# Long GpSimd operations moved to VectorE and ScalarE, modulation weights as overlapping 128-row tiles, and a new order, in an adaLN block with dilated sliding attention

## The chip, the cores and the metric

The kernel runs on one core of one Trainium2 chip. Its five engines are TensorE (PE, matmuls), VectorE (DVE), ScalarE (ACT), GpSimd (POOL) and SyncE (SP); transfers run on DMA queues that SP and ACT issue. The metric is device time in microseconds (us) of one execution; lower is better. Three runs of the kernel before took 187.68 to 190.51 us, median 189.6.

## What is computed

`x` has 2048 rows of D = 448 bf16 values. A condition vector `c` (1 x 448) gives six modulation vectors.

```python
mod = (silu(c) @ w_mod).reshape(1, 6, 1, 448)     # sa, ca, ga, sb, cb, gb
h = layernorm(x) * (1 + ca) + sa
q, k, v = heads(h @ wqkv)                         # 16 heads of 28
# each position attends to 8 positions: itself and 2, 4, ... 14 before it
x = x + ga * (softmax(q k^T / sqrt(28)) v @ wo)
h = layernorm(x) * (1 + cb) + sb
x = x + gb * (silu(h @ w1) @ w2)                  # 448 -> 1792 -> 448
```

## The kernel before

The rows are split by parity (even and odd positions never attend to each other) into two sequences of NP = 1024, and these into NC = 4 chunks of 256. A first stage loads everything, takes the layer norm of each pair of 128-row tiles (`n10` to `n17`; `n1m` is pair m), transposes and modulates it into `hT` (`h0` to `h3` by chunk), and projects q and k (`qk<chunk><group>`) and v (`v0` to `v8`). Attention runs over nine units u of two blocks of 57 queries and 64 keys: logits `lg`, two exponentials `ex`, a mask `mk` on VectorE that multiplies the 1824 values of each row, weighted sums `av`, a reciprocal `rc` and a product `on`, a DMA transpose `otr` on SP, and a copy `al` that places the result in `oT`. Then follow the output projection `wo0` to `wo7` with its residual `res`, the second norms `n20` to `n27`, and the feed-forward part in four steps `s0` to `s3`: `f1` (448 to 1792, SiLU on ACT) and `f2` (1792 to 448), with the sum `ya` and the store `sto`.

TensorE works with pairs of 64-row halves: each projection has a part `S`, a GpSimd no-op that signals its end, and a part `C`. Four PSUM tiles of two banks (`ps`) are shared by all stages; whoever wants one waits for the reader of its last content.

The order of all 640 operations is written out by hand in the table `ORDER`: a number is the operation, the letter its engine (p TensorE, v VectorE, a ScalarE, g GpSimd, s SyncE). Each engine executes its own in that order, so an operation that waits holds up all that stand behind it on that engine. `hT` and `oT` are two ranges of one tile `ho`, so an `al` copy and a projection that follows it in the table also wait for each other.

At the start the modulation weights `w_mod` lie as four blocks of KM = 112 rows. The weights of q and k arrive in two halves, `ldwqk0` (row blocks 0, 1) and `ldwqk1` (2, 3); `pad0` to `pad3` copy them into `wp` with 32 columns per head; `mod1` is the matrix product that gives sa and ca. The first projection needs all four pads, the four modulations `h00.mod0`, `h00.mod1`, `h01.mod0`, `h01.mod1`, and so all of that. GpSimd does the small norm steps (`rstd`: one or two operations on 128 x 2 values, `nm`, `mean`), the signals, and before the change also two pads, two of nine `al` copies, one of two gatings of `wo` (`wog0`) and four of seven gatings of `w2` (`w2g`), which multiply the weights by ga and gb. Second norms take their sums from the residual (`accum_out`), and the squares on ACT (`HOW2`, "s"); first norms use VectorE's batch-norm statistics ("b").

Of the kernel before, what the change touches and what calls it, by code (L numbers as in the profile page):

```python
# [882 lines left out]
```

## Time and profile before

| | |
|---|---|
| three runs | 187.68, 189.6, 190.51 us |
| the profiled execution, its own time | 186.92 us |
| its span (first to last instruction) | 185.1 us |
| TensorE busy in the span | 162.3 us (88%) |
| VectorE, ScalarE, GpSimd busy | 93.7, 96.2, 44.7 us |
| mean granted TensorE clock | 0.979 |

Busy times say how long an engine executed, and not what the kernel waited for. For that the stretches in which TensorE sat idle are looked at, what ended each, and what that operation had waited for itself. A time such as 39.42 is a start counted from the span's begin.

### The profile page before, as it was taken

The page shows a single profiled execution, that of the slowest core. Times are in us where ns is not written, and L with a number is a line of the kernel's source. Part 1 is how long each engine was busy: PE and PEld are TensorE (multiplying, and loading weights), DVE is VectorE, ACT ScalarE, POOL GpSimd, SP SyncE. Part 2 cuts the span into 40 slices and gives each one's busy share as a digit, 9 for nine tenths or more (in the row PEclk, how much of TensorE's full clock was granted, in tenths as well). Part 3 has the DMA queues.
Part 4 walks back from the last instruction along what each step waited for, and adds up shares of the span by engine and source line. Part 5 has one row for each costly group of instructions (what it writes and reads, how often), then busy time and mean ns, then how long its engine had stood idle before and what let it go on. Part 6 is the DMA issues. An engine that isn't in the chain of part 4 may idle for free.

```text
span 185.1 us, 6152 instructions
## 1 busy us (share of the span) xinstructions
PE 162.3 (88%) x2713; PEld 84.8 (46%) x2713; DVE 93.7 (51%) x194; ACT 96.2 (52%) x128; POOL 44.7 (24%) x91
## 2 busy tenths in 40 slices
PE   7979799677868989879999999999999999999910
PEld 2344354354334545545556644455444445554700
DVE  2879999679557858993327484032062000002620
ACT  2140598725259657586698785585338854200000
POOL 6346434551100059432304202000400000000000
PEclk9999999997899999999999999999999999999995
DMA  5993599999687956434003343900009000000132
GB/s 176 339 360 84 96 200 239 110 132 119 210 62 197 212 199 31 89 75 102 0 0 60 64 104 68 109 0 4 0 3 259 4 0 4 0 0 4 50 102 66
DMA packets 33114, 18.20 MB, mean 98 GB/s; under 512 B 25016, under 2 KB 32568, under 8 KB 33080
## 3 DMA queue, kind: packets, MB, share of 16 engines
q1 hardware_dynamic: 30752, 14.92, 40.7%
q10 hardware_dynamic: 2328, 2.81, 4.9%
q8 instruction: 23, 0.38, 0.9%
q14 instruction: 11, 0.09, 0.2%
HBM read 9.86 MB, written 1.84 MB: 63 GB/s over the span
## 4 chain that ended last, share of the span: by engine, by line
PE 70%; DVE 8%; DMA 6%; POOL 5%; ACT 3%; issue 2%; DVEq 0%; POOLq 0%; ACTq 0%
PE ps L682 23%; PE ps L707 20%; PE ps L473 10%; PE ps L653 5%; DMA wqk<-in_A_wqkv_dram 4%; PE ps L490 4%; PE ps L719 3%; PE ps L602 2%; PE ps L528 2%; POOL rs L372 2%; DMA x_all<-in_A_x_dram 2%; DVE xn L387 1%; ACT ho L236 1%; DVE st L356 1%; DVE p L586 1%
## 5 line engine op out<-in xcount | busy, mean ns | idle before, releaser
L707 PE MATMUL ps<-w,both 64*128 64x448 bf16 x392 | 38.9, 349 | 0.0
L687 ACT ACTIVATE both<-ps 128x1024 bf16<-128x1024 f32 x28 | 27.8, 1022 | 17.6 <-PE ps L682 17.2
L473 PE MATMUL ps<-ho,wp 64*128 64x512 bf16 x224 | 26.9, 385 | 3.9 <-POOL ho L623 1.4
L682 PEld LDWEIGHTS <-w 64*128 64x128 bf16 x392 | 20.0, 94 | 22.5 <-issue 1.0
L707 PEld LDWEIGHTS <-both 64*128 64x128 bf16 x392 | 19.0, 94 | 17.6
L682 PE MATMUL ps<-h,w 64*128 64x512 bf16 x196 | 22.5, 376 | 0.6 <-ACT v L495 0.6
L682 PE MATMUL ps<-wqk,w 64*128 64x512 bf16 x196 | 22.3, 376 | 0.0
L661 DVE SCALAR_TENSOR_TENSOR x_all<-ps,x_all 128x448 bf16<-128x448 f32 x16 | 9.3, 621 | 22.6 <-PE ps L653 22.6
L473 PEld LDWEIGHTS <-wp 64*128 64x128 bf16 x224 | 11.3, 95 | 17.3 <-issue 3.8
L535 ACT ACTIVATE p<-ps 128x912 bf16<-128x912 f32 x18 | 15.9, 929 | 5.4 <-PE ps L528 5.3
L742 DVE TENSOR_TENSOR wqk<-ps,x_all 128x896 bf16<-128x896 f32 x3 | 3.3, 1087 | 26.8 <-issue 26.8
L490 PE MATMUL ps<-wv,ho 64*64 64x448 bf16 x252 | 14.8, 352 | 1.8 <-issue 1.4
L477 ACT CAST qk<-ps 128x1024 bf16<-128x1024 f32 x11 | 10.5, 1016 | 7.9 <-PE ps L473 7.9
L387 DVE TENSOR_SCALAR xn<-x_all,mv,rs 128x512 bf16<-128x512 bf16 x26 | 12.4, 509 | 4.2 <-POOL rs L372 4.2
L364 POOL TENSOR_SCALAR mv<-sums 128x2 f32<-128x2 f32 x8 | 3.0, 376 | 41.8 <-DVE x_all L661 34.3
L653 PE MATMUL ps<-wo,ho 64*128 64x448 bf16 x112 | 12.8, 350 | 0.0
L367 ACT ACTIVATE scr<-x_all,mv 128x448 bf16<-128x448 bf16 x16 | 10.6, 664 | 3.8 <-POOL mv L364 3.5
L586 DVE TENSOR_TENSOR p<-p,maskb 128x1824 bf16<-128x1824 bf16 x9 | 11.7, 1299 | 1.7 <-ACT p L535 1.7
L356 DVE BATCH_NORM_STATS2 st<-x_all 128x6 f32<-128x448 bf16 x16 | 9.9, 619 | 2.7 <-DMA x_all<-in_A_x_dram 2.7
L614 DVE TENSOR_TENSOR o<-ps,rc 121x896 bf16<-121x896 f32 x9 | 9.8, 1086 | 0.7 <-DMA op<-o 0.5
L490 PEld LDWEIGHTS <-ho 64*64 64x64 bf16 x252 | 7.1, 106 | 6.5 <-issue 4.0
L293 PE MATMUL ps<-junk 64*128 64x512 bf16 x56 | 9.0, 488 | 1.2 <-DVE junk L203 1.2
(84 smaller groups left out, 175.7 us busy)
## 6 DMA issues: line engine op xcount, KB each, us to landing
w<-in_B_w_dram SPq DMA_DIRECT2D x2, 896.0 KB, 6.0
w<-in_B_w_dram SPq DMA_DIRECT2D x2, 784.0 KB, 5.9
x_all<-in_A_x_dram SPq DMA_DIRECT2D x2, 448.0 KB, 10.0
out_dram<-ot SPq DMA_DIRECT2D x4, 224.0 KB, 2.2
both<-in_w_mod_dram ACTq DMA_DIRECT2D x1, 784.0 KB, 8.5
wo<-in_A_wo_dram SPq DMA_DIRECT2D x2, 392.0 KB, 6.0
both<-in_w_mod_dram SPq DMA_DIRECT2D x1, 784.0 KB, 9.3
out_dram<-wqk SPq DMA_DIRECT2D x3, 224.0 KB, 2.3
```

What stands on the lines that cost most here:

```text
L356: V.bn_stats(out=st[:], in_=x_all[:, us[t], :])
L367: S.activation(out=scr[:], in_=x_all[:, us[t], :], func=ACTF.Square, bias=mv[:, t, 0:1], accum_out=mv[:, t, 1:2])
L387: (V if o["eng"] == "dve" else G).tensor_scalar(out=out_, in0=in_, scalar1=mv[:, t, 0:1], scalar2=rs[:, t:t + 1], op0=ALU.subtract if b el ...
L473: return [matmul(t[:, j, :], lhsT=w, rhs=hT[rows, :, kt, s0:s0 + CP], start=start, stop=stop)]
L477: copy_on(o)(out=qk[:, :, g, :, s0:s0 + CP], in_=t[:].rearrange("p j (t s) -> p j t s", t=2))
L490: return [matmul(t[half(par), j, 0:D], lhsT=hT[rows, par, kt, k0:k0 + KB], rhs=wv[rows, kt, :], start=start, stop=stop) for par in range(2)]
L535: S.activation(out=p_of[u][:, 2 * t * w:2 * t * w + 2 * w].rearrange("p (j n) -> p j n", j=2), in_=bank(a, t)[:, :, 0:w], func=ACTF.Exp, s ...
L586: V.tensor_tensor(out=p, in0=p, in1=m, op=ALU.mult)
L653: x = matmul(t[:, par, 0:D], lhsT=oT[rows, par, i // 2, 128 * m:128 * m + 128], rhs=wo[rows, j, :], start=(j == 0), stop=(j == 5))
L682: return [matmul(t[:, i // 7, :], lhsT=w1[rows, kt, 128 * i:128 * i + 128], rhs=h[rows, :, kt, :], start=start, stop=stop)]
L687: S.activation(out=hid[:, k % 2, :, i, :], in_=t[:], func=ACTF.Silu)
L707: x = matmul(t[:, par, 0:D], lhsT=hid[half(hf), k % 2, jj, ii, 128 * j:128 * j + 128], rhs=w2[half(hf), ii + 7 * jj, :], start=(way == 0 a ...
```

## The change

- GpSimd gives up everything long but memsets: the pads, the `al` copies and the gatings run on VectorE or ScalarE only.
- `w_mod` lies as four tiles of 128 rows: rows 0 to 383 as three, and rows 320 to 447 as the fourth, whose first 64 rows meet zeros in `scT`. It is loaded in four transfers that all stages share, two for sa and ca, two for the rest. `c` is loaded as 7 rows of 64.
- The four second norms `n24` to `n27` use batch-norm statistics on VectorE ("b") and no squares on ACT. The addition of EPS moves from VectorE into GpSimd's `rstd`, which always has two operations now. `nm` and `mean` may run on VectorE, and `nm` is left out where VectorE does the normalisation.
- The whole of `ORDER` is another one, also for the transfers.

The core of the diff (the table is left out: its rows below tell what moved):

```diff
-HOW2 = "ssssssss"
+HOW2 = "ssssbbbb"
...
     def load_mod(name, c0, c1):
-        return dma(name, f"ldm{(c1 - c0) // D}", wmod[:, :, c0:c1], w_mod.rearrange("(k p) n -> p k n", p=KM)[:, :, c0:c1])
+        n = (c1 - c0) // D
+        return [dma(f"{name}0", f"ldm{n}x3", wmod[:, 0:3, c0:c1], w_mod[0:384, c0:c1].rearrange("(k p) n -> p k n", p=128)),
+                dma(f"{name}1", f"ldm{n}x1", wmod[:, 3, c0:c1], w_mod[320:448, c0:c1])]
...
-    ld_ma = load_mod("ldm_sa", 0, 2 * D)
+    ld_ma = load_mod("ldm_a", 0, 2 * D)
...
-    ld_mo, ld_mb, ld_m2 = load_mod("ldm_ga", 2 * D, 3 * D), load_mod("ldm_sb", 3 * D, 5 * D), load_mod("ldm_gb", 5 * D, 6 * D)
+    ld_mo = ld_mb = ld_m2 = load_mod("ldm_b", 2 * D, 6 * D)
...
                 V.bn_aggr(out=mv[:, t, :], in_=st[:])
-                V.tensor_scalar(out=mv[:, t, 1:2], in0=mv[:, t, 1:2], scalar1=EPS, scalar2=None, op0=ALU.add)
...
             def rstd(o):
-                if not b:
-                    G.tensor_scalar(out=rs[:], in0=mv[:, :, 1], scalar1=1.0 / D, scalar2=EPS, op0=ALU.mult, op1=ALU.add)
-                G.tensor_tensor(out=rs[:], in0=mv[:, :, 1] if b else rs[:], in1=negh[:], op=ALU.pow)
+                G.tensor_scalar(out=rs[:], in0=mv[:, :, 1], scalar1=1.0 if b else 1.0 / D, scalar2=EPS, op0=ALU.mult, op1=ALU.add)
+                G.tensor_tensor(out=rs[:], in0=rs[:], in1=negh[:], op=ALU.pow)
...
-    pads = [P.op(f"pad{kt}", "vag", "pad", lambda o, kt=kt: pad(o, kt), [ld_qk[kt // 2]]) for kt in range(KT)]
+    pads = [P.op(f"pad{kt}", "va", "pad", lambda o, kt=kt: pad(o, kt), [ld_qk[kt // 2]]) for kt in range(KT)]
...
-        al_done[u] = P.op(f"al{u}", "vag", "align", align, [trs] + late)
+        al_done[u] = P.op(f"al{u}", "va", "align", align, [trs] + late)
...
-            wo_gated = [P.op(f"wog{i}", "vg", "wog", lambda o, i=i, n=n: eng[o["eng"]].tensor_tensor(out=wo[:, i:i + n], in0=wo[:, i:i + n],
+            wo_gated = [P.op(f"wog{i}", "v", "wog", lambda o, i=i, n=n: eng[o["eng"]].tensor_tensor(out=wo[:, i:i + n], in0=wo[:, i:i + n],
...
-            w2_gated = [P.op(f"w2g{f}", "vg", "w2g", lambda o, f=f: eng[o["eng"]].tensor_tensor(out=w2[:, f:f + 2, :], in0=w2[:, f:f + 2, :],
+            w2_gated = [P.op(f"w2g{f}", "v", "w2g", lambda o, f=f: eng[o["eng"]].tensor_tensor(out=w2[:, f:f + 2, :], in0=w2[:, f:f + 2, :],
```

Three places of the order. First VectorE at the start, before the first projection. In the kernel before, `xn` are the normalised tiles, `wp` a pad, `modc` the modulation vectors (from `mod1`), `ho` from `ps` the first chunk's modulations:

```order
L387 TENSOR_SCALAR xn_80<-x_all,mv,rs 128x512 x2
L387 TENSOR_SCALAR xn_81<-x_all,mv,rs 128x512 x2
L305 COPY screp<-scT 112x512
L432 COPY wp<-wqk 128x32x28
L321 COPY modc<-ps_112 128x4
L322 TENSOR_SCALAR modc<-ps_112 128x4
L238 TENSOR_SCALAR ho<-ps_111,modc 128x2x128 x2
L238 TENSOR_SCALAR ho<-ps_110,modc 128x2x128 x4
```

and in the changed kernel:

```order
L358 BN_STATS st<-x_all 128x6
L359 BN_AGGR mv<-st 128x2
L392 TENSOR_SCALAR xn_81<-x_all,mv,rs 128x512 x2
L437 COPY wp<-wqk 128x32x28
L323 COPY modc<-ps_112 128x4
L324 TENSOR_SCALAR modc<-ps_112 128x4
L237 TENSOR_SCALAR ho<-ps_111,modc 128x2x128 x2
L237 TENSOR_SCALAR ho<-ps_110,modc 128x2x128 x2
L237 TENSOR_SCALAR ho<-ps_111,modc 128x2x128 x2
```

The pad of VectorE still stands ahead of the modulation vectors, but it is now `pad1`, whose weights are the half that is loaded last (before it was `pad0` of the half that was loaded first). Second SyncE's queue at the start, before:

```order
L241 DMA x_all<-in_A_x_dram 128x896
L241 DMA wqk<-in_A_wqkv_dram 128x2x896
L241 DMA x_all<-in_A_x_dram 128x2x896
L241 DMA wv<-in_A_wqkv_dram 128x2x448
L241 DMA x_all<-in_A_x_dram 128x2x896
```

and changed:

```order
L240 DMA x_all<-in_A_x_dram 128x896
L240 DMA wqk<-in_A_wqkv_dram 128x2x896
L240 DMA c_67<-in_c_dram 7x64
L240 DMA x_all<-in_A_x_dram 128x2x896
L240 DMA both<-in_w_mod_dram 128x896
L240 DMA wqk<-in_A_wqkv_dram 128x2x896
L240 DMA x_all<-in_A_x_dram 128x2x896
L240 DMA wv<-in_A_wqkv_dram 128x2x448
```

Both halves of the q and k weights are on this queue now; before, the second was the fourth transfer of ACT's. Third VectorE around the gating of `wo` and the first `al` copies; in the changed kernel (`p` from `p` and `maskb` is a mask, `ho` from `op` an `al` copy; before, the first two `al` were on GpSimd and ACT, and the first `wo` row on GpSimd):

```order
L591 TENSOR_TENSOR p_93<-p_93,maskb 128x1824
L787 TENSOR_TENSOR wo<-wo,gbc 128x1792
L614 RECIPROCAL rc<-ps_112 121x32
L619 TENSOR_TENSOR o_96<-ps_112,rc 121x2x448
L237 TENSOR_SCALAR ho<-ho,modc 128x2x256 x4
L787 TENSOR_TENSOR wo<-wo,gbc 128x1344
L323 COPY modc<-ps_111 128x4
L324 TENSOR_SCALAR modc<-ps_111 128x4
L392 TENSOR_SCALAR xn_83<-x_all,mv,rs 128x512 x2
L591 TENSOR_TENSOR p_94<-p_94,maskb 128x1824
L628 COPY ho<-op_78 128x8x114
L628 COPY ho<-op_79 128x8x114
```

Both gatings and both copies are in VectorE's queue, the copies behind the mask of unit 2.

## Rows read from the trace of the kernel before

**Rows 1.** Busy time by stretch: stretch, length, each engine's busy time (instructions), granted clock, DMA share, GB/s

```profile
14.65:30.00 15.35, 13.53 (x262) 6.74 (x264) 14.56 (x44) 8.93 (x10) 6.40 (x17) 1.00 0.64 133
30.00:45.00 15.00, 10.95 (x326) 6.10 (x330) 12.34 (x22) 8.83 (x11) 8.37 (x10) 0.97 1.09 136
45.00:60.00 15.00, 12.06 (x347) 6.17 (x348) 9.62 (x12) 8.99 (x12) 1.30 (x1) 0.92 0.75 158
60.00:81.75 21.75, 19.15 (x528) 11.10 (x525) 18.36 (x30) 14.29 (x22) 11.14 (x13) 1.00 0.64 127
81.75:176.46 94.71, 94.68 (x1154) 49.31 (x1154) 28.26 (x59) 51.45 (x70) 9.86 (x24) 1.00 0.20 41
```

**Rows 2.** Waits of TensorE: line, what it waited for, us, times, longest

```profile
PE ps L473 <- POOL ho L623: 1.4, 1, 1.4
PE ps L490 <- issue: 1.4, 2, 0.9
PE ps L528 <- DVE qk L477: 1.3, 1, 1.3
...
PE ps L528 <- issue: 1.2, 2, 1.1
PE ps L335 <- DVE v L495: 1.2, 1, 1.2
PE ps L473 <- ACT ho L623: 1.0, 1, 1.0
PE ps L602 <- DVE o L614: 1.0, 1, 1.0
PE ps L473 <- POOLq L218: 0.9, 1, 0.9
```

**Rows 3.** Timeline, VectorE then GpSimd: start, us, line, operation, count

```profile
29.98 1.10 DVE L586 TENSOR_TENSOR p<-p,maskb 128x1824 bf16<-128x1824 bf16 x1
...
39.42 3.20 DVE L238 TENSOR_SCALAR ho<-ho,modc 128x512 bf16<-128x512 bf16 x1
...
30.14 2.15 POOL L372 TENSOR_TENSOR rs<-mv,negh 128x2 f32<-128x2 f32 x2 [3.20 <-DVE mv L358]
...
38.90 3.57 POOL L782 TENSOR_TENSOR wo<-wo,gbc 128x1792 bf16<-128x1792 bf16 x1 [3.61 <-PE ps L490]
```

**Rows 4.** By tile and by line: ns minimum/median/maximum, first and last start

```profile
L356 DVE BATCH_NORM_STATS2 st<-x_all x16: 614/618/628, 4.2 to 31.0; 128x6 f32<-128x448 bf16 x16
L387 DVE TENSOR_SCALAR xn<-x_all,mv,rs x26: 394/408/1956, 8.0 to 137.1; 128x512 bf16<-128x512 bf16 x26
L238 DVE TENSOR_SCALAR ho<-ho,modc x8: 399/408/3199, 24.9 to 44.6; 128x512 bf16<-128x512 bf16 x8
L586 DVE TENSOR_TENSOR p<-p,maskb x9: 1099/1124/2015, 30.0 to 102.3; 128x1824 bf16<-128x1824 bf16 x9
L784 DVE TENSOR_TENSOR w<-w,gbc x3: 553/554/619, 77.6 to 90.5; 128x896 bf16<-128x896 bf16 x3
```

**Rows 5.** Chain that ended last, at the start: start, us, what

```profile
4.42 8.31 DMA wqk<-in_A_wqkv_dram
...
12.79 1.82 POOL wp L432 x2
...
14.65 5.57 PE ps L473 x50
```

**Rows 6.** Transfers issued from 2.5 to 3.0 us: KB, us to landing

```profile
x_all<-in_A_x_dram SPq DMA_DIRECT2D x1, 448.0 KB, 10.0
```

**Rows 7.** Timeline of ACT and VectorE up to the first projection

```profile
9.20 0.94 ACT L432 COPY wp<-wqk 128x896 bf16<-128x896 bf16 x1 [0.78 <-issue]
12.52 1.02 ACT L236 ACTIVATE ho<-ps,modc 128x256 bf16<-128x256 bf16 x2 [2.38 <-DVE ho L238]
...
11.69 2.00 DVE L238 TENSOR_SCALAR ho<-ps,modc 128x256 bf16<-128x256 bf16 x6
```

**Rows 8.** Busy time of one more stretch, columns as in rows 1

```profile
45.60:50.00 4.40, 4.38 (x103) 1.72 (x88) 2.14 (x4) 1.75 (x2) 0.00 (x0) 0.79 0.89 249
```

More of the change, by code (lines that the diff above doesn't have):

```diff
@@ L21 @@
 KT = 4
-KM = D // KT
 NP = 1024
@@ L296, in layer @@
     P.release(junks, w_first, "ps")
-    sc_op = P.op("silu_c", "a", "silu_c", lambda o: S.activation(out=sc4[:], in_=c4[:], func=ACTF.Silu), [ld_c, tab])
+    sc_op = P.op("silu_c", "a", "silu_c", lambda o: S.activation(out=sc7[:], in_=c7[:], func=ACTF.Silu), [ld_c, tab])
     def c_cols(o):
-        matmul(bank(o)[0:KM, 0, 0:KT], lhsT=sc4[:], rhs=ident[0:KT, 0:KT], start=True, stop=True)
+        for hf, c0, n, at, step in ((0, 0, 3, 0, 2), (0, 8, 1, 3, 1), (1, 1, 3, 0, 2), (1, 6, 1, 3, 1)):
+            matmul(bank(o)[half(hf), 0, at:at + n], lhsT=sc7[:], rhs=ident[0:7, c0:c0 + step * (n - 1) + 1:step], start=True, stop=True)
     cc = P.op("ccol", "p", "ccol", c_cols, [sc_op], take=("ps",), group=("F", None, 0))
-    sct = P.op("scT", "av", "tiny", lambda o: copy_on(o)(out=scT[:], in_=bank(cc)[0:KM, 0, 0:KT]), [cc])
+    sct = P.op("scT", "av", "tiny", lambda o: copy_on(o)(out=scT[:], in_=bank(cc)[:, 0, 0:KT]), [cc])
     P.release([sct], cc, "ps")
-    rep = P.op("screp", "vg", "screp", lambda o: copy_on(o)(out=screp[:], in_=scT[:].unsqueeze(2).to_broadcast([KM, KT, 128])), [sct])
+    rep = P.op("screp", "v", "screp", lambda o: copy_on(o)(out=screp[:], in_=scT[:].unsqueeze(2).to_broadcast([128, KT, 128])), [sct])
     ROW = (0, 128, 192, 320)
@@ L322, in ev @@
             V.tensor_scalar(out=modc[:, dst0 + 1, :], in0=t[:, 1, :], scalar1=1.0, scalar2=None, op0=ALU.add)
-        a = P.op(f"{name}.mm", "p", "modcol", mm, [sct, load], take=("ps",), group=("F", None, 0))
+        a = P.op(f"{name}.mm", "p", "modcol", mm, [sct] + load, take=("ps",), group=("F", None, 0))
         e = P.op(f"{name}.ev", "v", "modev", ev, [a])
@@ L335, in mm @@
                 matmul(bank(o)[:, 0, 0:D], lhsT=screp[:, k, :], rhs=wmod[:, k, v * D:(v + 1) * D], start=(k == 0), stop=(k == KT - 1))
-        a = P.op(f"{name}.mm", "p", "gate", mm, [rep, load], take=("ps",), group=("F", None, 0))
+        a = P.op(f"{name}.mm", "p", "gate", mm, [rep] + load, take=("ps",), group=("F", None, 0))
         wmod_read.append(a)
@@ L363, in mean @@
             def mean(o):
-                G.tensor_scalar(out=mv[:, :, 0], in0=sums[:, us[0]:us[0] + 2], scalar1=-1.0 / D, scalar2=None, op0=ALU.mult)
+                (V if o["eng"] == "dve" else G).tensor_scalar(out=mv[:, :, 0], in0=sums[:, us[0]:us[0] + 2], scalar1=-1.0 / D, scalar2=None, op0=ALU.mult)
             def square(o, t):
@@ L369, in rstd @@
             def rstd(o):
[L370 to L372 removed]
+                G.tensor_scalar(out=rs[:], in0=mv[:, :, 1], scalar1=1.0 if b else 1.0 / D, scalar2=EPS, op0=ALU.mult, op1=ALU.add)
+                G.tensor_tensor(out=rs[:], in0=rs[:], in1=negh[:], op=ALU.pow)
             def shift(o):
+                if all(x["eng"] != "act" for x in self.xn):
+                    return
+                if o["eng"] == "dve":
+                    V.scalar_tensor_tensor(out=nm[:], in0=mv[:, :, 0], scalar=-1.0 if b else 1.0, in1=rs[:], op0=ALU.mult, op1=ALU.mult)
+                    return
                 G.tensor_tensor(out=nm[:], in0=mv[:, :, 0], in1=rs[:], op=ALU.mult)
```

60 lines of the change are left out of this document (30 added, 30 removed).

## The prediction

> **What bounds the kernel now.** I read busy time by stretch first. From 81.75 us on, TensorE is busy for 94.68 of 94.71 us [rows 1]; nothing that other engines do there sets the end, as long as they keep up. The end of the span, 185.1, follows 8.64 us after the last of that work, and I change nothing there. So the question is when TensorE gets to 81.75. Its first projection starts at 14.65 [rows 5], and between the two lie 67.10 us, in which it is busy for 13.53 + 10.95 + 12.06 + 19.15 = 55.69 [rows 1]. It idles 11.4 us in the attention part, and that is what an order can win.
>
> Next the waits of TensorE [rows 2]. The eight rows there sum to 9.4, and what is left of the 11.4 are short ones. The two rows that name "issue" (1.4 and 1.2) are waits that nothing in the profile ends; the change does not touch them. The other 8.8 us wait for VectorE, ScalarE or GpSimd, which deliver late.
>
> Why late: GpSimd's gating of `wo` ran from 38.90 for 3.57 us, and the VectorE modulation that started beside it at 39.42 took 3.20 us, until GpSimd was done [rows 3]. The same instruction takes 0.41 us elsewhere [rows 4]. VectorE's `xn` and mask show the same maxima, 1.96 and 2.02 us against medians of 0.41 and 1.12 [rows 4]. These three alone held VectorE for 2.79 + 1.55 + 0.89 = 5.2 us, in stretches in which it was busy for 12.3 of 15 and 18.4 of 21.75 us [rows 1]. Behind the first stood the v evacuation for which TensorE waited 1.2 us. Two more waits, 1.4 and 1.0 us, are for `al` copies on GpSimd and ACT [rows 2].
>
> **The change, step by step** (minus is gain).
>
> *Waits that go: -8.8.* GpSimd keeps no instruction of this length but its memsets, so VectorE's stretched operations go back to their medians; the `al` copies of units 0 and 1 and the evacuation at the 1.3 us wait change engines; the signals for which TensorE waited 0.9 us stand behind one norm's steps and no longer behind two norms'. Each of the waits of rows 2 but "issue" loses its cause; what takes their place is counted next. Bounds: 0 if every one is only replaced, -8.8.
>
> *What VectorE takes over* costs seven gatings of `w2` instead of three, 4 x 0.55 = 2.2 us [rows 4], a gating of `wo` of 1792 columns (twice a 896-column one, 1.1), and three `al` copies at about the 0.41 of a modulation, an estimate [rows 4]. That is 4.5 us against at least 5.2 of stretching that goes, and 16 additions of EPS that go too. So VectorE's load in the attention part hardly changes, and I cost it at nothing in total, but not in place:
>
> *New waits: +2.0.* The order puts `al0` on VectorE behind two `xn` and the mask of unit 2, and TensorE's `qk21.C` stands behind `al0`. After chunk 2 is modulated VectorE has 2 x 0.41 + 1.12 [rows 4] and the copy to do, 2.3 us with 0.4 for the copy, and the rest of `wo`'s gating; TensorE has `qk21.S` and one block of logits. I take 1.3, between 0 (TensorE comes later for another reason) and 2.3. Later `qk30.S` waits for `al3`, and `wo2.S` for an evacuation that now stands behind a mask and that copy; 0.7 together, between 0 and two masks, 2.2.
>
> *Short GpSimd operations: +0.8.* All sixteen `rstd` stay on GpSimd and have two steps each now. Beside VectorE's mask at 29.98 (1.10 us) two of their steps took 2.15 us together [rows 3], so blocking goes the other way too. I take 0.8, near a single case of it, between 0 and four cases (four of the second norms lie on the way to the first feed-forward step), 4 x 1.1 = 4.4, of which most would be hidden.
> The Trainium skill has a rule that speaks against the move here: SBUF — State Buffer, "Who interferes with whom", says that VectorE and GpSimd share a port pair by an exclusive lock, that a VectorE instruction with two SBUF inputs counts too against a GpSimd one that reads SBUF, and that the order of issue decides who waits. By it the gatings that move (two SBUF inputs) turn from blockers of VectorE into blockers of GpSimd's norm steps, so that the lock's loss shrinks and does not vanish. The 3.20 us and the 2.15 us rows agree with it; with no rule the sum would be 0.8 lower.
>
> *The start: +1.5.* Before, the second half of the q and k weights landed at 4.42 + 8.31 = 12.73, GpSimd's two pads took 1.82, and the projection began at 14.65 [rows 5], 1.92 after landing. Now the last half is `ldwqk0`, sixth on SyncE's queue. The transfers up to its end are 224 + 448 + 1 + 448 + 224 + 448 KB, about 1,792. The chunk of x that ended SyncE's 224 + 448 + 448 + 224 + 448 = 1,792 KB before landed 10.0 us after an issue between 2.5 and 3.0 [rows 6], so at 12.5 to 13.0; ACT's queue is as full beside it as before (224 + 672 + 448 + 448 KB). I take 12.73 again, between 11.2 and 13.7. Then `pad0` on ACT takes 0.94, `h00.mod1` behind it on ACT 1.02, and only then come `h00.mod0` and `h01.mod0` on VectorE (they write into the same tile, and the first waits for ACT), two thirds of 2.00, 1.33 [rows 7]. With 0.15 for the hand-overs: 12.73 + 3.44 = 16.2 against 14.65. The new `pad1` on VectorE holds up the modulation vectors too, but ACT's pad is longer. For a landing at 11.2 the term is 0, for 13.7 it is 2.5.
>
> *Clock: -0.5.* In 45.60 to 50.00 the granted clock was 0.79, so part of it at the lower of the two levels, after a stretch in which TensorE was busy for 10.95 of 15 us [rows 8, 1]. There it did 24 projection matmuls and one unit's 64 small ones in 4.38. By 5.57 us for 50 [rows 5] the 24 take 2.7, so that at most 1.7 less the time of the small ones is lost; I take 1.0. With denser work it comes back, unless the gap ahead of the first projection costs as much: -0.5, bounds -1.0 and +1.0.
>
> *Feed-forward part: +0.3.* Four norms with statistics on VectorE add 8 x 0.62 = 5.0 us [rows 4] and the short aggregations to it, where it has 94.71 - 28.26 idle [rows 1], and take 8 squares from ACT; hidden. What could show is that stats, `al7` and transposes stand in one line: `n25`'s statistics behind `al7`, which waits for a DMA transpose that SyncE issues behind a store. By the order TensorE has work for about 1 us longer than that chain and the one to `f130.S` take; if that cover is gone, every us shows. 0.3, bounds 0 and 2. One unit's sums (`av6`) moves behind the first feed-forward step; that is the same work later. The four transfers of `w_mod` and its 128-row matmuls are as many as before and I cost them at nothing; the larger second pair lands before its first use, since it is issued about 10 us ahead and the queues are empty by then.
>
> Sum: -8.8 + 2.0 + 0.8 + 1.5 - 0.5 + 0.3 = **-4.7 us**. Against the profiled execution's own 186.92 that is 182.2; it lies 2.7 below the median of the runs shown (189.6), so against the median 184.9. I predict 184.9, 2.5% less.
>
> **The rivals.**
> *All of it clears.* No new waits, no blocking; the weights land at about 12, +0.7. -8.8 + 0.7 - 0.5 = -8.6: 181.0. For it: VectorE's load falls by as much as it takes over. Against: each of the two engines waits for the other in turn, and TensorE's idle time before was made of ten small causes and not of one.
> *VectorE becomes the bound.* It was busy for 14.56 of 15.35 us in the first stretch and 18.36 of 21.75 in the last [rows 1], and every new copy stands in its one line. New waits at their upper bound (4.5 instead of 2.0) and blocking at 2.0: -4.7 + 2.5 + 1.2 = -1.0: 188.6. Against: the stretched instructions are part of that busy time.
> *The clock falls at the start* (slower than before). After the last warming matmuls TensorE has nothing for about 2 us until 16.2; if the clock is then granted at the lower level for the whole first chunk, its 50 matmuls take 5.57 longer [rows 5], and the 0.5 is not won: -4.7 + 5.6 + 0.5 = +1.4: 191.0. It decides from 4.7 us of loss on. For it: rows 8 show that gaps cost clock. Against: there the lower level cost 1.0 us, and the start before, with gaps too, kept 1.00 [rows 1].
>
> **How the numbers follow.** Likeliest (183 to 187.5): 0.42; all clears (179 to 183): 0.20; VectorE bound (187.5 to 190): 0.27; clock (190 to 194): 0.11. The range 180.5 to 190.0 leaves out the last and about 0.06 of the second. About 2% can be told from no change here: below 185.8 lie the second case and 0.36 of the first, 0.56; above 193.4 about 0.06 of the last and of what I have not thought of; between them 0.38.
>
> **What the changed profile would show.** Right: VectorE's modulation, `xn` and mask with maxima near their medians; the first projection at about 16; TensorE's idle time between it and the first feed-forward matmul at 5 to 6 us, with `al0` the largest named wait; that matmul at about 76 to 77; no idle time after. Wrong: a first projection at 14.7 or earlier (the landing), a granted clock below 1 in 14 to 25, waits of TensorE for VectorE of over 5 us, or idle time after the first feed-forward step.

## The result, and the profile after the change

The changed kernel takes 181.18 us (median of four runs, 180.88 to 181.69) against 188.64 us (187.11 to 190.51) of the kernel before beside it: a ratio of 0.963 (95% interval 0.955 to 0.972). A second comparison gave 0.959 (0.950 to 0.967). The forecast, 184.9, had the sign right, and the result lies inside its range, but the gain is 7.5 us where it said 4.7.

| | before | after |
|---|---|---|
| profiled execution, its own time | 186.92 us | 180.88 us |
| its span | 185.1 us | 179.0 us |
| first matmul of the first projection | 13.74 us | 13.37 us |
| first feed-forward matmul (f1) | 81.75 us | 74.16 us |
| TensorE idle from there to f1 | 11.5 us | 6.5 us |
| end of TensorE's long work | 176.46 us | 170.35 us |

Busy time by stretch of the kernel after (columns as in [rows 1], to which these answer):

```profile
13.37:30.00 16.63, 12.99 (x304) 7.24 (x307) 12.71 (x29) 10.94 (x13) 5.04 (x13) 0.97 1.02 244
30.00:45.00 15.00, 13.99 (x368) 7.68 (x361) 11.75 (x25) 9.76 (x12) 1.97 (x4) 0.92 0.62 75
45.00:60.00 15.00, 14.80 (x372) 7.95 (x372) 11.12 (x26) 8.43 (x13) 1.12 (x3) 1.00 0.69 131
60.00:74.16 14.16, 12.54 (x395) 7.44 (x369) 11.34 (x21) 8.29 (x13) 0.93 (x2) 1.00 0.67 180
74.16:170.35 96.19, 95.57 (x1219) 48.15 (x1218) 34.72 (x79) 49.26 (x59) 6.96 (x16) 1.00 0.21 40
```

The 14.65 us of [rows 5], from which the prediction and [rows 1] count, are not the start of the first projection before. Six of its 56 matmuls had run by then, from 13.74 on; 14.65 is where the other 50 go on, when GpSimd's second pad is done. So not all of that projection needs all four pads. The first line is that projection before, from a timeline (start, us, engine, line, operation); the other two are the stretch from its first matmul to the first f1, before and after, with the columns of [rows 1]:

```profile
13.74 6.48 PE L473 MATMUL ps<-ho,wp 64*128 64x512 bf16 x56
```

```profile
13.74:81.75 68.01, 56.51 (x1456) 30.30 (x1453) 55.61 (x104) 41.04 (x53) 28.07 (x42) 0.97 0.77 140
```

```profile
13.37:74.16 60.79, 54.32 (x1391) 30.31 (x1391) 46.91 (x98) 37.42 (x48) 9.06 (x22) 0.97 0.76 159
```

The feed-forward stretch is 1.48 us longer, 0.89 of it work that moved there (95.57 against 94.68). So the span's 6.1 us come from a start 0.37 earlier, 5.0 less idle time in the attention part and 1.3 less busy time for the same matmuls, less 0.6 of new idle time behind the first f1. Where the 1.3 lies the rows do not show; the granted clock, 0.97 over both stretches, does not give it.

The waits of TensorE after (line, releaser, us, times, longest), the answer to [rows 2]:

```profile
PE ps L533 <- DVE v L500: 2.8, 1, 2.8
PE ps L478 <- DVE ho L628: 1.6, 2, 1.1
...
PE ps L607 <- issue: 1.0, 1, 1.0
...
PE ps L607 <- DVE p L591: 0.6, 1, 0.6
PE ps L687 <- DVE w L789: 0.5, 1, 0.5
```

Of the waits in rows 2 that for `al0` is left, now on VectorE, and "issue"; the others are gone. L628 is the forecast waits, for `al0` (1.1) and `al3` (0.5). The largest was not foreseen. Its place, on VectorE and TensorE (timeline: start, us, engine, line, operation, idle time before and its releaser):

```profile
26.17 0.73 DVE L237 TENSOR_SCALAR ho<-ho,modc 128x512 bf16<-128x512 bf16 x2 [3.65 <-DMA ho<-xn]
26.82 1.08 DVE L500 CAST v<-ps 128x896 bf16<-128x896 f32 x1
...
27.96 0.70 PE L533 MATMUL ps<-qk 28*64 28x57 bf16 x64 [2.82 <-DVE v L500]
```

TensorE wants the logits of unit 1 and needs the PSUM tile that `v0.ev` empties (L500); that stands on VectorE behind chunk 1's modulations, which waited for DMA transposes. Last, durations by tile (ns minimum/median/maximum), the answer to [rows 4]:

```profile
L392 DVE TENSOR_SCALAR xn<-x_all,mv,rs x21: 380/408/414, 7.1 to 132.1; 128x512 bf16<-128x512 bf16 x21
...
L237 DVE TENSOR_SCALAR ho<-ho,modc x11: 317/409/414, 26.2 to 56.5; 128x512 bf16<-128x512 bf16 x11
...
L591 DVE TENSOR_TENSOR p<-p,maskb x9: 1090/1119/1125, 28.1 to 96.1; 128x1824 bf16<-128x1824 bf16 x9
...
L372 POOL TENSOR_TENSOR rs<-rs,negh x16: 690/700/1040, 6.1 to 131.0; 128x2 f32<-128x2 f32 x16
```

VectorE's maxima of 3.20, 1.96 and 2.02 us are gone: not one of its modulations, normalisations or masks is held. The memsets that stay on GpSimd can still hold it: a copy for `screp` at 17.93 took 1.26 us beside a memset of 1.00 at 17.91, and 0.39 in the second execution.

Three of the variants below (a_pool, b_dve, a_w112) were profiled in a slow execution, at a lower granted clock, so of these traces only durations, waits and transfer rates are read; ratios compare fast runs alone (of a_pool's ten these are three), while a median in us is over all runs.

### The profile page after: what moved, and what is told of

Same layout as the page of the kernel before. It is cut to its first block, busy times and chain, and to the rows that moved or that the text cites. A ratio compares the mean times of both kernels' runs of the same rounds, so it can differ in the third digit from the quotient of the medians.

```text
span 179.0 us, 6114 instructions
## 1 busy us (share of the span) xinstructions
PE 160.5 (90%) x2716; PEld 83.5 (47%) x2716; DVE 92.3 (52%) x206; ACT 92.8 (52%) x115; POOL 23.6 (13%) x65
## 4 chain that ended last, share of the span: by engine, by line
PE 57%; DMA 20%; DVE 13%; issue 3%; POOL 1%; SPq 1%; ACT 1%; ACTq 0%; DVEq 0%; POOLq 0%
PE ps L687 19%; PE ps L712 16%; DMA ho<-xn 8%; PE ps L478 7%; PE ps L658 6%; DMA op<-o 5%; DMA wqk<-in_A_wqkv_dram 3%; PE ps L724 3%; DMA wqk<-xn 3%; PE ps L607 2%; PE ps L495 2%; DMA x_all<-in_A_x_dram 2%; DVE o L619 2%; DVE ot L747 2%; DVE st L358 2%
## 5 line engine op out<-in xcount | busy, mean ns | idle before, releaser
L687 PEld LDWEIGHTS <-w 64*128 64x128 bf16 x392 | 19.0, 94 | 23.1 <-issue 0.8
L478 PE MATMUL ps<-ho,wp 64*128 64x512 bf16 x224 | 27.3, 388 | 2.0 <-DVE ho L628 1.6
L478 PEld LDWEIGHTS <-wp 64*128 64x128 bf16 x224 | 11.4, 96 | 14.8 <-issue 3.5
L482 ACT CAST qk<-ps 128x1024 bf16<-128x1024 f32 x12 | 11.8, 1013 | 9.4 <-PE ps L478 9.4
L358 DVE BATCH_NORM_STATS2 st<-x_all 128x6 f32<-128x448 bf16 x24 | 14.6, 609 | 3.4 <-DMA x_all<-in_A_x_dram 3.4
L747 DVE TENSOR_TENSOR wqk<-ps,x_all 128x896 bf16<-128x896 f32 x2 | 2.2, 1087 | 24.7 <-PE ps L712 24.7
L495 PE MATMUL ps<-wv,ho 64*64 64x448 bf16 x252 | 13.3, 351 | 0.0
L371 POOL TENSOR_SCALAR rs<-mv 128x2 f32<-128x2 f32 x16 | 3.5, 217 | 70.8 <-DVE st L358 20.6
L392 DVE TENSOR_SCALAR xn<-x_all,mv,rs 128x512 bf16<-128x512 bf16 x21 | 7.9, 406 | 8.6 <-POOL rs L372 8.6
L372 POOL TENSOR_TENSOR rs<-rs,negh 128x2 f32<-128x2 f32 x16 | 11.6, 722 | 1.3
L591 DVE TENSOR_TENSOR p<-p,maskb 128x1824 bf16<-128x1824 bf16 x9 | 10.0, 1115 | 0.1
L747 DVE TENSOR_TENSOR ot<-ps,x_all 128x896 bf16<-128x896 f32 (+2 forms) x8 | 6.5, 852 | 6.5 <-PE ps L724 4.3
## 6 DMA issues: line engine op xcount, KB each, us to landing
both<-in_w_mod_dram ACTq DMA_DIRECT2D x1, 1344.0 KB, 10.1
```

Source lines behind the costliest of these rows:

```text
L358: V.bn_stats(out=st[:], in_=x_all[:, us[t], :])
L372: G.tensor_tensor(out=rs[:], in0=rs[:], in1=negh[:], op=ALU.pow)
L478: return [matmul(t[:, j, :], lhsT=w, rhs=hT[rows, :, kt, s0:s0 + CP], start=start, stop=stop)]
L482: copy_on(o)(out=qk[:, :, g, :, s0:s0 + CP], in_=t[:].rearrange("p j (t s) -> p j t s", t=2))
L495: return [matmul(t[half(par), j, 0:D], lhsT=hT[rows, par, kt, k0:k0 + KB], rhs=wv[rows, kt, :], start=start, stop=stop) for par in range(2)]
L687: return [matmul(t[:, i // 7, :], lhsT=w1[rows, kt, 128 * i:128 * i + 128], rhs=h[rows, :, kt, :], start=start, stop=stop)]
```

## The experiments

Every ratio below is to the kernel before, run beside each variant on the same chip. In a_pool, b_dve, a_qklate and a_modlate the table is wrapped over more lines, so that every line number is 22 higher than in the kernel that was edited (L500 of a_qklate is L478 of the changed kernel).

**The changed kernel again** (no edit).

> The changed kernel once more, unaltered, beside the kernel before and the other variants on one chip. Theory 1: the ratio to the kernel before is a property of the two programs; it is 0.963 again, 180.5 to 182 us. Theory 2: part of the 3.7% came from the chip or the hour of the first comparison (four runs each, the kernel before from 187.1 to 190.5): the ratio is 0.97 to 0.985, and the variants are then to be read against that.

Measured: 180.13 us, ratio 0.959 (0.950 to 0.967). The gain belongs to the programs. But its trace is not the first one's: the projection starts at 14.10, the wait for `v0.ev` is 0.5 us, and in the middle of unit 3's logits TensorE stands 1.2 us for "issue"; idle time in the attention part is 4.1 us. Single waits shift by 1 to 2 us between executions of one program; their sum is what to compare.

**Seven long operations back on GpSimd** (a_pool; 153 is `wog0`, 155, 156, 158, 160 are gatings of `w2`, 258 and 323 `al0` and `al5`), and **the same seven off GpSimd in the kernel before** (b_dve).

```diff
 after.py, ORDER
-153v ... 258v ... 155v 156v ... 158v ... 323v ... 160v
+153g ... 258g ... 155g 156g ... 158g ... 323g ... 160g
 before.py, ORDER
-153g ... 258g ... 160g ... 158g ... 155g ... 156g ... 323g
+153v ... 258v ... 160v ... 158v ... 155v ... 156v ... 323v
```

> The changed kernel with seven long operations back on GpSimd at their places in the order: the first gating of wo, four gatings of w2 (w2g0, w2g2, w2g6, w2g10) and the copies al0 and al5. Theory 1, the long GpSimd operations hold VectorE (before, three VectorE instructions were held 5.2 us in sum): VectorE's modulations, xn or masks show maxima of 2 to 3 us again, and the time rises by 2 to 4 us over the changed kernel's 181.2. Theory 2, the order made the gain and the place of the long operations does not matter: VectorE has 4 x 0.62 + 1.08 + 2 x 0.40 = 4.4 us less to do, and the time stays within 1 us of 181.2.

> The kernel before, in its own order, with the same seven operations moved from GpSimd to VectorE. Theory 1 (long GpSimd operations hold VectorE): the modulation that took 3.20 us takes 0.41, the maxima of xn and mask fall to 0.41 and 1.12, and the time falls by 2 to 4 us from 188.6. Theory 2 (the order is what counts): VectorE gets 4.4 us more to do in an order that was not made for it, and the time changes by less than 1 us either way. Theory 3 (VectorE becomes the bound, as it was busy for 14.56 of 15.35 us in the first stretch and 18.36 of 21.75 in the last): slower by 1 to 3 us.

Measured: a_pool 189.72 us, ratio 1.000 (0.992 to 1.008): the whole gain is gone, more than either theory said. b_dve 187.97 us, ratio 1.000 (0.995 to 1.006): nothing is won. The rows of a_pool in the feed-forward part:

```profile
81.71 6.44 POOL L811 TENSOR_TENSOR w<-w,gbc 128x896 bf16<-128x896 bf16 x3
...
84.51 1.90 DVE L613 TENSOR_TENSOR p<-p,maskb 128x1824 bf16<-128x1824 bf16 x1
86.33 3.58 DVE L811 TENSOR_TENSOR w<-w,gbc 128x896 bf16<-128x896 bf16 x2
...
89.41 0.58 POOL L387 TENSOR_SCALAR mv<-sums 128x2 f32<-128x2 f32 x1
...
90.02 0.67 ACT L390 ACTIVATE scr<-x_all,mv 128x448 bf16<-128x448 bf16 x1 [4.14 <-POOL mv L387]
...
91.74 0.61 PE L709 MATMUL ps<-h,w 64*128 64x512 bf16 x4 [2.40 <-ACT both L714]
```

Three gatings take 6.44 us on GpSimd (0.62 each on VectorE), and beside them VectorE's mask takes 1.90 and its own two gatings 3.58: each engine holds the other. So theory 1 of a_pool is right in kind. But the 2.40 us for which TensorE waits do not come from holding alone: ScalarE, which it waits for, had stood idle 4.14 us for a norm step of GpSimd at 89.41, and that step stood in GpSimd's line behind the three gatings and `al5`. In b_dve the holding is nearly gone too (one `xn` still takes 1.59), and still there is no gain; its VectorE and TensorE show why:

```profile
50.55 0.85 DVE L804 TENSOR_TENSOR wo<-wo,gbc 128x1344 bf16<-128x1344 bf16 x1
51.32 1.12 DVE L608 TENSOR_TENSOR p<-p,maskb 128x1824 bf16<-128x1824 bf16 x1
52.35 1.08 DVE L804 TENSOR_TENSOR wo<-wo,gbc 128x1792 bf16<-128x1792 bf16 x1
53.35 0.40 DVE L645 COPY ho<-op 128x912 bf16<-128x912 bf16 x1
...
53.80 3.02 PE L495 MATMUL ps<-ho,wp 64*128 64x512 bf16 x14 [2.97 <-DVE ho L645]
```

`al0` (L645) now stands behind two gatings and a mask, 3.05 us, and TensorE waits 2.97 us for it.

**The same, with `al0` ahead of those three** (b_dve_al; 184 and 180 are `qk21.S` and `qk20.S`, 154 `wog4`, 290 the mask of unit 3).

```diff
-154v 290v 184p 180p 153v 258v
+184p 180p 258v 154v 290v 153v
```

> The kernel before with the seven long operations on VectorE as in the variant b_dve, and al0 on VectorE ahead of the gating wog4, the mask of unit 3 and the gating wog0 instead of behind them (qk21.S and qk20.S written ahead of it). Theory 1: taking the long operations off GpSimd gave nothing there because al0 then stood in VectorE's queue behind 3.0 us of other work, and TensorE waited 3.0 us for it; with al0 ahead that wait falls below 0.5 and the time falls by 2 to 3.5 us against b_dve and the kernel before, to about 185. Theory 2: the wait moves on to the next operation of VectorE's queue (masks, gatings, the copies of units 1 and 2): within 1 us of b_dve.

Measured: 186.01 us, ratio 0.980 (0.967 to 0.992). Theory 1: the 2.97 us wait is down to 0.5. Taking the long operations off GpSimd is worth about 2% in the old order, half of the gain, and only if the order of VectorE is mended with it.

**Only the two of the attention part back on GpSimd** (a_pool_at).

```diff
-153v ... 258v
+153g ... 258g
```

> The changed kernel with only wog0 and al0 back on GpSimd, the two long operations that lie in the attention part; the gatings of w2 stay on VectorE. Theory 1: the contention in the attention part is what the change removes: chunk 2's modulations take 2.9 instead of 1.4 us beside wog0, al0 takes 1.7 instead of 0.4 and TensorE waits for it, and the granted clock falls behind that wait; 2 to 4 us over the changed kernel, ratio 0.97 to 0.985. Theory 2: most of what the seven operations cost lies in the feed-forward part (three gatings of w2 in 6.44 us, TensorE waiting 2.4 us there): under 1 us over the changed kernel, ratio below 0.967.

Measured: 182.21 us, ratio 0.971 (0.963 to 0.978), about 1% over the changed kernel's 0.963 and 0.959: 1.4 to 2.3 us. Four rows show the mechanism:

```profile
35.78 3.58 POOL L787 TENSOR_TENSOR wo<-wo,gbc 128x1792 bf16<-128x1792 bf16 x1 [3.91 <-PE ps L495]
...
38.23 2.25 DVE L237 TENSOR_SCALAR ho<-ho,modc 128x512 bf16<-128x512 bf16 x4 [0.42 <-DMA ho<-xn]
...
41.69 2.18 POOL L628 COPY ho<-op 128x912 bf16<-128x912 bf16 x1 [2.33 <-DVE modc L324]
...
43.92 3.17 PE L478 MATMUL ps<-ho,wp 64*128 64x512 bf16 x14 [1.74 <-POOL ho L628]
```

Beside `wog0` four modulations take 2.25 us (1.38 in the changed kernel); `al0` takes 2.18 on GpSimd, against 0.40 on VectorE, beside an `xn` (41.31) and the mask of unit 2 (41.96, 1.11); TensorE waits 1.74, and the 14 matmuls behind that wait take 3.17, at a granted clock of 0.50 (43.92 to 47.00), against 1.69 at 1.00 in the changed kernel. That slow stretch is not peculiar to the copy: in the second execution of the changed kernel the same 14 take 3.17 too (42.56), behind its stop in unit 3. Both theories hold a part: the attention part has 1.4 to 2.3 us of what the seven cost; that the feed-forward part has the rest is by subtraction.

**The last q and k weights later** (a_qklate; 7 is `ldwqk0`, 11 `ldx3`, 6 `ldwv1`).

```diff
-7s 3a 11s 6s
+3a 11s 6s 7s
```

> The changed kernel with ldwqk0 two places later on SyncE's queue, behind ldx3 and ldwv1 (448 + 224 KB). At the 390 to 405 GB/s that the trace of the changed kernel shows there, ldwqk0 lands 1.7 us later, at about 12.0 instead of 10.27, and the first projection starts at about 15.1 instead of 13.37. Theory 1, the start is on the path: the time rises by the same 1.7 us, to 182.9. Theory 2, the start is swallowed by TensorE's 2.8 us wait at 25.1 to 27.96, which ends with the transposes of chunk 1 and not with TensorE's own work: the wait shrinks by 1.7 us and the time stays within 0.4 us of 181.2.

Measured: 184.95 us, ratio 0.989 (0.985 to 0.994). The chain at the start and TensorE:

```profile
6.38 7.39 DMA wqk<-in_A_wqkv_dram
...
16.78 8.01 PE L500 MATMUL ps<-ho,wp 64*128 64x512 bf16 x56 [2.11 <-DVE ho L259]
```

The weights land at 13.77, 3.5 us later and not 1.7; the projection starts 3.4 us later, and the span grows by 3.5 (182.5). Theory 1: the start passes to the end in full. The wait for `v0.ev` is gone there, but in the same place, behind 59 of unit 1's 64 logits, TensorE stands 1.37 us for "issue" instead, so nothing of the later start is swallowed. My landing came from one queue alone, as in the prediction, and was too early here: `ldx2` (6.47) and `ldm_b1` (7.33), issued on ScalarE's queue, share the time.

**Modulation weights in 112-row tiles again** (a_w112), and **128-row tiles in the kernel before** (b_w128).

```diff
 after.py
-w_mod[0:384, c0:c1].rearrange("(k p) n -> p k n", p=128)
+w_mod[0:336, c0:c1].rearrange("(k p) n -> p k n", p=112)
-w_mod[320:448, c0:c1]
+w_mod[336:448, c0:c1]
 before.py
-w_mod.rearrange("(k p) n -> p k n", p=KM)[:, :, c0:c1]
+w_mod[0:384, c0:c1].rearrange("(k p) n -> p k n", p=128)   and   w_mod[320:448, c0:c1]
 both: c, scT, screp and the products to match
```

> The changed kernel with the modulation weights as four tiles of 112 rows again, in the same four transfers (336 and 112 rows) and the same order; c as 4 rows of 112. Theory 1 (bytes count): the four overlapping tiles carry 512 rows and these 448, so 2.41 MB instead of 2.75; at 390 GB/s the first pair is 0.3 us and all four 0.9 us shorter, in the stretch where the queues are full (share 1.02); the transposes of chunk 1 land about 0.9 us earlier and the time falls by 0.3 to 1. Theory 2 (rows count): the layout is worth nothing, or 112-row transfers and matmuls are slower (414 against 350 ns for the eight of ga and gb, 0.5 us in all): 0 to +1 us.

> The kernel before with the modulation weights as four overlapping tiles of 128 rows (each of its four loads as two transfers, 384 and 128 rows) and c as 7 rows of 64; its order and everything else as it was. Theory 1 (rows count): in 5 to 11 us the kernel before moved 335 GB/s and the changed one 384 at the same share of busy DMA time, and the changed kernel with 112 rows 316; with 128 rows the q and k weights land 0.5 to 1.5 us before 12.73 although 14% more bytes are loaded, the first projection starts at 13.3 to 14.2 instead of 14.65, and the time falls by 0.5 to 1.5 us (ratio 0.992 to 0.997). Theory 2 (bytes count): 112 KB more ahead of the weights, landing 0.3 us later, ratio 1.00 to 1.003.

Measured: a_w112 185.46 us, ratio 0.971 (0.960 to 0.983); b_w128 187.36 us, ratio 1.001 (0.997 to 1.005). Busy time in 5 to 11 us, one line each from before, after, a_w112 and b_w128 (the last two columns: DMA share, GB/s):

```profile
5.00:11.00 6.00, 4.51 (x53) 2.24 (x50) 4.86 (x17) 1.40 (x3) 2.94 (x8) 1.00 1.07 335
```

```profile
5.00:11.00 6.00, 4.87 (x76) 2.90 (x72) 4.86 (x17) 3.60 (x6) 3.35 (x7) 1.00 1.06 384
```

```profile
5.00:11.00 6.00, 5.00 (x65) 2.60 (x61) 3.97 (x13) 2.93 (x5) 2.56 (x6) 1.00 1.06 316
```

```profile
5.00:11.00 6.00, 3.65 (x62) 2.13 (x59) 5.08 (x17) 1.34 (x3) 2.64 (x8) 1.00 1.06 384
```

Rows count: with the same share of busy DMA time, 128-row tiles move 384 GB/s and 112-row tiles 316 to 335. In the changed kernel's order the 112-row form loses more by the rate than it saves in bytes: the last weights land at 11.06, 0.8 later. Its ratio lies 0.8 to 1.3% above the changed kernel's, with intervals that overlap, so that the layout's worth there is likely and not settled. In the kernel before, the weights landed at 12.2 instead of 12.73, and it won nothing. In the profiled execution 18 warming matmuls in front of the projection took 3.29 us instead of 2.12, and the projection began at 15.09 instead of 13.74; whether that is so in all ten runs is not shown.

**Later modulation weights** (a_modlate; 13 and 12 are `ldm_b1` and `ldm_b0`, 117 the second transpose of chunk 1, 149 and 147 the products gb and ga, 150 and 148 their evacuations, 259 the logits of unit 1, 127 `qk11.S`), and **with projections ahead of the first weighted sums** (a_modlate2; 135 is `qk13.S`, 254 `av0`, 121 `h1.mod2`, 260 and 261 the exponentials of unit 1, 256 `on0`).

```diff
 a_modlate
-13a ... 12a ... 117s ... 149p 147p 150a 259p 148v ... 127p
+117s 13s 12s ... 259p ... 127p 149p 147p 148v 150a
 a_modlate2, with the same two transfers, and then
-149p 147p 150a 259p 148v ... 254p 121a 135p 260a ... 261a ... 256v ... 127p
+259p ... 121a 260a 261a 135p 127p 254p 149p 150a 147p ... 256v ... 148v
```

> The changed kernel with the second pair of modulation weights (ldm_b, 1,344 and 448 KB) moved from ScalarE's queue at 9 to 11.7 us to SyncE's, behind the transposes of chunk 1, and the two matrix products that read them (ga, gb) moved behind the first projection part of chunk 1's second group. Theory 1, these 1.8 MB delay the transposes (8.85 us from issue to landing at 26.14, DMA share 1.02, against 3.2 us before): the transposes land by 22 to 23, TensorE's 2.8 us wait for v's evacuation falls below 0.6, and the time falls by 2 to 2.6 us, to about 178.8. Theory 2, the transposes are slow of themselves or wait for the other loads: they land after 25 as now, and the time stays within 0.5 us or rises, since the products wait for the later weights.

> The variant with the later modulation weights, and with qk13.S and qk11.S of chunk 1 ahead of the first weighted sums (av0); ga and gb behind av0. Theory 1: in the first variant the 2.8 us wait only changed its name: TensorE had 0.24 us of work in 25.0 to 27.3, waiting for the mask (0.8) and for 'issue' (1.5), and the granted clock in 27.3 to 31 was 0.56. With 16 to 32 projection matmuls in that place the gap closes and the clock stays at 1: first f1 matmul 2 to 3 us earlier than there, time 178 to 179.5. Theory 2: the 'issue' wait belongs to av0 wherever it stands and the projection waits for chunk 1's modulations instead: within 1 us of the first variant.

Measured: a_modlate 185.42 us, ratio 0.986 (0.979 to 0.992); a_modlate2 183.95 us, ratio 0.977 (0.969 to 0.985): the first slower than the changed kernel (0.963, 0.959), the second likely so, as its interval overlaps with one of those two. The transposes did land by 22.4, so 1.8 MB of weights were what delayed them, and the wait for `v0.ev` is gone. TensorE stopped at another thing. In a_modlate (its trace is of its fastest execution, 181.50 us), by stretch, and where it went on again:

```profile
25.00:27.30 2.30, 0.24 (x8) 0.14 (x11) 1.95 (x5) 2.24 (x3) 0.00 (x0) 0.96 1.00 398
27.30:31.00 3.70, 3.70 (x77) 1.76 (x76) 1.45 (x2) 0.00 (x0) 0.63 (x2) 0.56 0.57 138
```

```profile
27.26 0.94 PE L629 MATMUL ps<-v,p 64*57 64x29 bf16 x61 [1.47 <-issue]
```

and in a_modlate2, with other work in that place:

```profile
28.68 3.17 PE L478 MATMUL ps<-ho,wp 64*128 64x512 bf16 x13 [2.60 <-issue]
```

Both theories on a_modlate2 fail: the gap did not close, and it did not stay with `av0`; it is longer and has moved onto the projection. (The 13 matmuls behind it took 3.17 us at a granted clock of 0.50, as with the 0.56 above.)

**`v0.ev` and the mask ahead of the modulations** (a_v0first; 119, 120, 122 are modulations of chunk 1, 100 `v0.ev`, 253 `mk0`), and **with `al0` ahead of the mask of unit 2 and `ldwo1` later** (a_best).

```diff
 a_v0first
-119v 103p 122v 100v 120v 253v 104a 149p 147p 150a 259p 148v
+103p 100v 253v 104a 149p 147p 150a 259p 148v 119v 122v 120v
 a_best, beyond that
-15a ... 14s ... 276v 258v
+14s 15s ... 258v 276v
```

> The changed kernel with v0.ev, the mask of unit 0 (mk0) and ga.ev ahead of the three modulations of chunk 1 on VectorE instead of behind them or between them. Nothing else moves. Theory 1: TensorE's wait for v0.ev (2.8 us in the first profile of the changed kernel, 0.5 in the second) is a matter of VectorE's order: v0.ev and mk0 are ready at 22.5 and 24.2, but stand behind modulations that wait for the transposes, while VectorE idles 3.65 us. With them ahead, the logits lg1 and the sums av0 run in 25.1 to 26.7 and the projection of chunk 1 starts at 27 to 27.5 instead of 30.22 (28.36): 1 to 2.9 us less, a ratio of 0.945 to 0.955 to the kernel before, where the changed kernel had 0.963 and 0.959. Theory 2: the transposes are what TensorE waits for in the end, or the lead is used up by the next wait: ratio 0.957 to 0.965.

> The same, and two more: al0 on VectorE ahead of the mask of unit 2 instead of behind it, and ldwo1 (392 KB, first read at 36) from ScalarE's queue at 13.75 to SyncE's behind ldwo0, so that the transposes of chunk 1 have less traffic beside them. Theory 1: al0's wait (1.1 us in the first profile) and about 1 us of the transposes' 8.9 us go too: 1 to 2 us below the variant with v0.ev ahead, ratio 0.935 to 0.95. Theory 2: al0 waits for its own DMA transpose (landed at 44.2 of 44.75) and the transposes for the larger ldm_b: no more than the variant with v0.ev ahead.

Measured: a_v0first 179.65 us, ratio 0.957 (0.949 to 0.966); a_best 182.15 us, ratio 0.964 (0.955 to 0.973). The first is the fastest of all, but cannot be told from the changed kernel (0.959, 0.963). Its projection of chunk 1 starts at 26.96, 1.4 to 3.3 us before the changed kernel's two (28.36, 30.22), and its f1 at 71.73, 1.3 to 2.4 before theirs. In a_best the place where the wait was is as long as ever:

```profile
26.20 0.22 PE L533 MATMUL ps<-qk 28*64 28x57 bf16 x5 [0.42 <-issue]
```

```profile
29.96 0.27 PE L533 MATMUL ps<-qk 28*64 28x57 bf16 x5 [3.23 <-issue]
```

(a_v0first above, a_best below.) In both TensorE did 59 of unit 1's 64 logits, stopped, and did the other five later. By the ratios of both, theory 2 holds: the wait that was taken away gives nothing that can be told from no change.

## Why the prediction was right, and where its sum was wrong

**Where the time is.** Right: all of it came from before the first f1; the tail is 8.65 us against 8.64, and TensorE's idle time behind f1 is 0.6 us in 96.

**Long GpSimd operations as the cause.** Right, and shown in both directions by durations: VectorE's maxima vanish without them and come back with them (2.25 for 1.38, 1.90 for 1.12). But the prediction took the held time as the price. Runs b_dve and b_dve_al say that the removal alone is worth 0, and 2% with one copy put elsewhere. What it is worth is decided by what then stands in VectorE's line. Which of the other moves in the order bring the changed kernel from 0.980 to 0.96 was not tested one by one, nor were the second norms by batch-norm statistics.

**Waits that go, -8.8, and new ones, +2.0.** All of rows 2's waits for other engines did go or were replaced; but those sum to 6.8, and the other 2.0 of the 8.8 were short waits that no row names. The named new ones came out close: `al0` 1.1 for 1.3, the later two 0.5 for 0.7. Missed: 2.8 for `v0.ev` (0.5 in the second execution), 0.6 for a mask behind it. The prediction costed the larger second pair of modulation weights at nothing because it lands before its first use. It does; but it delays the transposes that run beside it, the last of them to 8.85 us from issue to landing (2.8 and 3.8 in a_modlate, without it). The other way, "issue", which the prediction held fixed at 2.6, fell to 1.0 in one execution and 2.2 in the other. Idle time forecast 5.4, measured 6.5 and 4.1.

**Short GpSimd operations, +0.8.** Mis-sized: the longest second step of an `rstd` took 1.04 us against a median of 0.70, and off the path. The rule of the Trainium skill weighed there (SBUF — State Buffer, "Who interferes with whom"), by which the order of issue decides who waits, agrees with a_pool_at where GpSimd's gating, issued first, held VectorE's modulations (2.25 for 1.38). GpSimd's copy there (2.18) ran beside an `xn` that was issued before it, but also beside a mask that VectorE issued after it, which the order of issue alone does not give.

**The start, +1.5: the step that failed.** The forecast was a projection at 16.2, measured is 13.37, and a_qklate shows that a later start counts in full. As a gain it is small, -0.4 from first matmul to first matmul (13.74 to 13.37; the first matmul behind the projection starts at 20.15 and 19.62), and -1.28 only by the 14.65 that the prediction counted from: the last half of the weights lands 2.46 earlier, but the kernel before could begin without it, and the changed kernel needs it first. The chain behind the landing was right, 3.10 us for a forecast 3.44:

```profile
4.35 5.92 DMA wqk<-in_A_wqkv_dram
10.27 0.02 issue
10.29 0.88 ACT wp L437
11.17 0.05 issue
11.21 0.42 ACT ho L235
...
12.27 1.37 DVE ho L237 x4
```

```profile
13.37 6.32 PE L478 MATMUL ps<-ho,wp 64*128 64x512 bf16 x56 [0.41 <-DVE ho L237]
```

What was wrong is the landing, 10.27 for a forecast 12.73 with bounds from 11.2. I had counted SyncE's queue to its sixth transfer, 1,792 KB in both kernels, and called ScalarE's queue "as full beside it". Counted over both queues by the time of issue, before had 3,249 KB issued up to the last half of the q and k weights (SyncE's 224, 448, 448, 224, 448; ScalarE's 224, 1, 784, 448), after 2,689 KB: ScalarE issues its third, `ldx2`, only at 6.33, behind the SiLU that waits for `c`. The rates from 3.0, when the queues run full, to each landing, before and after (last column):

```profile
3.00:12.73 9.73, 8.24 (x91) 4.09 (x89) 6.86 (x24) 2.10 (x5) 3.78 (x12) 1.00 1.06 356
```

```profile
3.00:10.27 7.27, 6.29 (x78) 3.13 (x74) 4.97 (x15) 2.90 (x6) 4.39 (x12) 1.00 1.06 390
```

So 3.33 MB at 356 GB/s from 3.0 give 12.3, and 2.75 MB at 390 give 10.1, close to the measured 12.73 and 10.27. By the same numbers about 1.6 us of the difference are bytes and 0.7 the rate. The rates are read from these same windows, so that this checks the count of bytes and forecasts nothing. In a_qklate the count falls short: 3.44 MB issued up to that load give about 11.9 by its rate of 385 GB/s, and it landed at 13.77, since transfers issued soon after it shared the time. So the count gives a lower bound. The Trainium skill says in DMA: Bandwidth & Descriptors, "Issuing engines are not separate DMA queues", that transfers of all engines run on the same 16 DMA engines and interleave. The traces agree (12.3 and 10.1 counted over both queues, for 12.73 and 10.27), and the prediction should have used it.

**Clock, -0.5, and the feed-forward part, +0.3.** The clock gave nothing. The granted clock is 0.97 over the attention part of both kernels, and the stretch at the lower of its two levels (1.2 of 2.4 GHz) is still there and only came earlier: before, 0.90 in 40 to 45 us and 0.76 in 45 to 50; after, 0.90 in 25 to 30 and 0.76 in 30 to 35. That is about 3.4 us at the lower level in either, or 1.7 us lost, where the prediction put the loss before at 1.0. In place of this term stand the 1.3 us less busy time, which no term foresaw. The feed-forward part measured +0.6.

**From the profile to the median.** The sum made -4.7 against the profiled 186.92, and 6.0 was measured there. The rest of the miss, 2.4 us, is that I let after's median stand 2.7 above its profiled time, as before's did. After's stands 0.3 above it (181.18 and 180.88). The spread of the kernel before was its own, and medians of more of its runs (187.7 of 31, 187.4 of 13, 188.97 of 7) lie below the 189.6 of the three.

**The signs that the prediction named.** Several of those for "wrong" came, though the time lies in the range: the projection at 13.37 (14.7 or earlier was named), 5.5 us of waits for VectorE in the first trace (over 5; 2.1 in the second), a granted clock of 0.92 from 14.10 to 20 in the second. The first f1 is at 74.16 and not at 76 to 77, and the largest wait is for `v0.ev` and not for `al0`. So the cause was right, and that the sum missed the profiled change by only 1.4 us is in part luck. The start, forecast 1.9 too late, and the 1.3 us less busy time would have made it 3.2; 1.0 us more idle time than forecast, the 0.5 of the clock and 0.3 in the feed-forward part took 1.8 of it back.

**The rivals.** "All of it clears" (181.0) gives the measured time, by another way: new waits did come, and the earlier start and the 1.3 us less busy time paid for them. VectorE did not become the bound. The clock at the start cost far less than that rival said: 16 warming matmuls took 1.90 us in one execution and 3.17 in another, with the projection at 13.37 and 14.10, 0.7 later.

## What to carry to other kernels

Moving an operation to the engine that is waited for pays only together with its place in that engine's line: ask what stands behind it, and who waits for that. All bytes issued before a load on all queues, by the time of issue, give a lower bound for when it lands, and what is issued soon after it makes it later; where a queue's issues stand behind computation on that engine, they are later than their order says. And a load that is early enough for its reader can still be too early for a small transfer beside it.

## What the runs showed that was not expected

**112 rows against 128.** At the same busy share (1.06 to 1.07) the DMA engines moved 316 to 335 GB/s where the modulation weights were tiles of 112 rows, and 384 with 128; changed in both kernels, it went both ways.

**TensorE stops at fixed places of its own program, each time just behind a transfer of instructions.** Behind the last matmul of `v1.C`, a_modlate and a_modlate2 do 64 logits and three more matmuls (weighted sums in one, projections in the other) and stop; a_v0first, a_best and a_qklate do the 8 of ga and gb and 59 logits and stop: 67 each time, whatever the instruction is, for 0.4 to 3.2 us, with no operation that the profile names to wait for. The stop at the 55th or 54th of unit 5's 64 weighted sums, about 1.0 us, is in the changed kernel, a_v0first and a_best alike. One of the DMA queues carries instructions, in 23 packets of 16 KB over a whole run; its line in the window from 27 to 28 us of a_best:

```profile
q8 instruction: 1, 0.02, 8.1%
```

That packet ends at 28.43 and TensorE goes on at 29.96. All 37 stops of TensorE of 0.3 us or more that the fourteen traces put down to "issue" end 1.2 to 1.6 us after such a packet has ended. So these are most likely waits for the next instructions; what the packets hold is inferred from the times. Full queues are not the condition: in a_qklate's stop (30.53 to 31.90) the queues moved 0 GB/s, in a_modlate's (25.0 to 27.3) 398. Why a packet comes when it does, and what would shorten these stops, was not tried. In the changed kernel the wait for `v0.ev` ended at 27.96, some 3 us after a packet that starts between 23 and 24 us, and no stop is seen there: the two may lie over each other, which would be why taking away that wait alone won little.
